# Sparse attention and a soft mixture of experts on one core: engine programs in a block, or in the main body

## The chip, the core and the metric

The kernel runs on one core of a Trainium2 chip. The core has five engines with an instruction stream each: PE (matrix products; its weight loads are shown as PEld), DVE (vector), ACT (activation functions), POOL and SP. They run on their own and meet through semaphores only. Transfers between the chip's memory and the core's are issued by SP, ACT and POOL and carried out by 16 DMA engines. The metric is the device time of one execution in microseconds (us).

## The reference

```python
# q, k, v: [8, 8, 576, 64]
scores = scale * np.matmul(q, k.transpose(0, 1, 3, 2))
mask_plain = (rel >= 0) & (rel < window)                  # window = 32
mask_dil = (rel >= 0) & (rel < window * dilation) & (rel % dilation == 0)   # dilation = 4
scores = np.where(masks, scores, -1e9)      # first 4 heads plain, last 4 dilated
attn = softmax(scores);  attn_out = np.matmul(attn, v)
x = attn_out.transpose(0, 2, 1, 3).reshape(4608, 512)
logits = x @ phi                            # 32 slots: 8 experts of 4
d = softmax over the 4608 tokens;  slot_input = d.T @ x
for e in range(8):
    slot_out[e] = np.maximum(slot_input[e] @ w1[e], 0.0) @ w2[e]
c = softmax over the 32 slots;     return c @ slot_out      # [4608, 512] f32
```

## The kernel before

The attention is done in eight units (two batches of one kind of head each). For each unit POOL issues the loads of q, k and v into one of three staging buffers (`stg`), PE transposes them and ACT copies the result to `TT`; PE forms the scores, ACT their exponentials, DVE the masks; PE multiplies by the values, DVE divides, PE transposes again and forms the logits. The experts' weights, 32 MB in f32, are fetched through POOL's queue all along, into buffers as they come free (`WD`, `stg`, `TT`), and cast to bf16 on the way. At the end the two products of each expert run on PE, the outputs are formed in `WD` and `stg` by ACT (L1062) and DVE (L1061), and they are stored by SP, a few by ACT (L1056).

The whole program is recorded first. A call of `op` adds a step with its engine, what it reads and writes, a cost and a key; `P.schedule` gives each engine an order from these; `P.emit` then writes the instructions, one engine after the other. Nothing of this order depends on where `emit` writes them.

`emit` (L276) takes `eng_of`, which gives for each engine something that is called with a function and runs it with that engine (used as a decorator). Inside, every step's waits are written ahead of it and its semaphore is raised behind it (`c_pe`, `c_act` and so on; each transfer has its own).

Before, `eng_of` holds the decorators of a `Block` (L1167). A block gives every engine a stretch of program of its own: in the listing of the built program each engine has one `UnconditionalBranch` from the main body into its stretch (L314) and one at its end to the block's end (L1177). SP has two stretches, the second for the waits on the stores, with a branch between them (L1172). At the block's end stands a barrier of all five engines: PE, ACT, DVE and SP each drain and add one to a gathering semaphore; POOL drains, waits until it holds four, and adds four to a releasing semaphore, which each of the others waits for and counts down. All instructions of this barrier are shown under L1177. A barrier of the same form, with L1192 as its line, stands at the head of the program, before the block, and is written by the language, not by the kernel.

`s_out` (L416) lists the semaphores of the 18 stores. The last thing that SP does ahead of the closing barrier is to wait for each of them (L1174 and L1175). Other engines don't wait for the stores; they meet SP in the closing barrier.

The lines that matter below: L462, L516 and L532 (the first loads and ACT's first instruction), L495 (weight loads by POOL), L1056 (stores), L1175 (waits for the stores), L1177 (branches to the end and closing barrier), L1192 (opening barrier).

Of the kernel before, what the change touches and what calls it, by code (L numbers as in the profile page):

```python
# [327 lines left out]
def bass_dilated_sliding_attn__then__soft_moe_slots_kernel(  # L328
# [10 lines left out]
    A = es.enter_context  # L339
    P = Prog()  # L340
# [75 lines left out]
    s_out = []  # L416
# [575 lines left out]
    COLS, d_ = [], 0  # L992
# [156 lines left out]
    def filler(n):  # L1149
        t = tile(psum, 1)  # L1150

        def pe(te):
            for _ in range(n):
# [11 lines left out]

    P.schedule(filler, FILL)

    blk = A(nc.Block())
    P.emit(nc, {"pe": blk.tensor, "act": blk.scalar, "dve": blk.vector,
                "pool": blk.gpsimd, "sp": blk.sync})  # L1170

    @blk.sync  # L1172
    def _(sp):
        for d_ in s_out:  # L1174
            sp.wait_ge(d_.sem, d_.val)  # L1175

    es.close()  # L1177
    return nc
# [28 lines left out]
```

## Time and profile before

| | us |
|---|---|
| median of 3 runs (lowest, highest) | 176.54 (176.09, 176.54) |
| the profiled execution, its own time | 176.33 |
| its span, first to last instruction | 174.6 |
| busy: PE, DVE, ACT, POOL | 129.6, 110.4, 96.2, 65.3 |

The span runs from the first instruction of the kernel's program to the end of its last; the time of an execution also holds what lies around it, here 1.7 us. In the profile's 40 slices (4.4 us each) a digit is the busy share in tenths. A row of the chain of waits gives start, length and what the time went to; a row of waits gives the time waited in all, how often, and the longest. An engine's name with a q is its sequencer: waits, branches, drains and the issuing of transfers, which don't count as busy. The trace also holds the single instructions with their starts in nanoseconds, and the semaphore events with theirs, including those of the program that the launch puts around the kernel's own.

### The profile page before, as it was taken

To read this page: it belongs to the slowest core of one execution; us is meant where nothing else is said; L and a number is where in the kernel's file an instruction comes from. 1 tells how busy PE (TensorE), PEld (TensorE's weight loads), DVE (VectorE), ACT (ScalarE), POOL (GpSimd) and SP (SyncE) were. 2 spreads that over 40 slices of the span, in tenths; PEclk is the share of its full clock that TensorE was granted. 3 is DMA by queue.
4 is the path that set the end of the run, shared out by engine and by line. 5 is a ranking of instruction groups with operands and counts; after the bars stand their busy time and mean duration, and the time that the engine had idled before them with its cause. 6 is when DMAs were issued, how large, how long until landed. Compare 5 with 4: busy or idle time off the path is not lost.

```text
span 174.6 us, 5117 instructions
## 1 busy us (share of the span) xinstructions
PE 129.6 (74%) x2234; PEld 99.3 (57%) x2235; DVE 110.4 (63%) x259; ACT 96.2 (55%) x147; POOL 65.3 (37%) x111
## 2 busy tenths in 40 slices
PE   0057778989898999997989899978599856589000
PEld 0056668968686977885977797765454413333000
DVE  6620199299869899969789979996401102499200
ACT  2324743797978769797768696763101101589300
POOL 7980668404964033952020769498000000000000
PEclk9999996999999999999999999999957999999855
DMA  5999998999999999999999999999999999999997
GB/s 178 252 213 213 220 232 187 222 209 214 229 222 199 219 209 216 237 203 206 221 207 218 212 216 216 216 220 214 212 207 208 206 196 197 290 347 404 452 420 300
DMA packets 12693, 41.28 MB, mean 236 GB/s; under 512 B 2208, under 2 KB 8864, under 8 KB 9120
## 3 DMA queue, kind: packets, MB, share of 16 engines
q0 software_dynamic: 8128, 30.41, 86.6%
q1 hardware_dynamic: 2912, 8.98, 13.3%
q10 hardware_dynamic: 1632, 1.57, 2.7%
q8 instruction: 17, 0.28, 0.6%
q14 instruction: 4, 0.03, 0.0%
HBM read 61.93 MB, written 9.44 MB: 409 GB/s over the span
## 4 chain that ended last, share of the span: by engine, by line
PE 34%; DMA 23%; ACT 13%; DVE 13%; POOL 5%; issue 3%; ACTq 1%; POOLq 0%
DMA TT<-in_moe_w_dram 17%; PE ps L636 8%; PE ps L642 7%; DMA stg<-in_v_dram 6%; ACT PT L695 5%; DVE XB L753 4%; PE ps L713 4%; ACT WD L1062 4%; PE ps L742 4%; PE ps L688 4%; DVE PT L703 4%; PE ps L797 3%; PE ps L770 3%; ACT TT L670 3%; POOL TT L495 2%
## 5 line engine op out<-in xcount | busy, mean ns | idle before, releaser
L695 ACT ACTIVATE PT<-ps 128x768 bf16<-128x768 f32 x48 | 36.9, 819 | 11.5 <-PE ps L688 11.2
L670 ACT ACTIVATE TT<-ps 128x864 f32<-128x864 f32 x32 | 27.9, 901 | 17.6 <-PE ps L642 9.0
L753 DVE TENSOR_TENSOR XB<-ps,RV 96x768 bf16<-96x768 f32 x32 | 30.1, 944 | 0.4
L642 PE MATMUL ps<-ident,stg 96*128 96x96 bf16 x288 | 16.9, 225 | 12.7 <-DMA stg<-in_v_dram 12.0
L718 DVE COPY VN<-ps 128x768 bf16<-128x768 bf16 x32 | 17.1, 543 | 9.8 <-PE ps L713 9.5
L642 PEld LDWEIGHTS ps<-ident,stg 96*128 96x128 bf16 x288 | 15.4, 109 | 13.5 <-DMA stg<-in_v_dram 12.2
L742 PE MATMUL ps<-VN,PT 128*128 128x65 bf16 x384 | 17.3, 195 | 2.8 <-DVE XB L753 1.7
L688 PE MATMUL ps<-TT 64*128 64x96 bf16 x384 | 16.5, 213 | 3.2 <-ACT PT L695 1.2
L1062 ACT ACTIVATE WD<-ps,rtok 128x256 f32<-128x256 f32 (+1 forms) x22 | 10.5, 554 | 13.9 <-PE ps L1079 12.6
L713 PE MATMUL ps<-ident,TT 128*128 128x128 bf16 x192 | 17.1, 228 | 1.0 <-issue 0.3
L609 POOL COPY stg<-stg 96x576 f32<-96x576 f32 x24 | 16.8, 702 | 1.5
L742 PEld LDWEIGHTS ps<-VN,PT 128*128 128x128 bf16 x384 | 14.5, 99 | 4.2 <-DVE XB L753 1.9
L688 PEld LDWEIGHTS ps<-TT 64*128 64x128 bf16 x384 | 10.3, 98 | 8.7 <-ACT PT L695 2.3
L703 DVE TENSOR_TENSOR PT<-PT,mask_d 128x768 bf16<-128x768 bf16 x24 | 14.0, 616 | 0.0
L770 PE MATMUL ps<-ident,XB 96*128 96x96 bf16 x192 | 12.2, 211 | 2.2 <-DVE XB L753 1.5
L713 PEld LDWEIGHTS ps<-ident,TT 128*128 128x128 bf16 x192 | 11.8, 102 | 3.3 <-issue 1.1
L703 DVE TENSOR_TENSOR PT<-PT,mask_p 128x768 bf16<-128x768 bf16 x24 | 12.6, 544 | 0.2
L448 POOL DMA_DIRECT2D stg<-in_q_dram x8 | 4.1, 525 | 21.7 <-PE ps L642 21.7
L770 PEld LDWEIGHTS ps<-ident,XB 96*128 96x128 bf16 x192 | 9.5, 101 | 4.2 <-DVE XB L753 2.8
L636 PE MATMUL ps<-ident,stg 96*128 96x96 bf16 x216 | 11.2, 212 | 0.0
L783 ACT ACTIVATE XT<-ps 128x576 bf16<-128x576 bf16 x16 | 10.0, 651 | 1.6 <-PE ps L770 1.4
L636 PEld LDWEIGHTS ps<-ident,stg 96*128 96x128 bf16 x216 | 10.5, 102 | 0.4
(99 smaller groups left out, 204.0 us busy)
## 6 DMA issues: line engine op xcount, KB each, us to landing
WD<-in_moe_w_dram POOLq DMA_DIRECT2D x6, 1024.0 KB, 25.9
stg<-in_moe_w_dram POOLq DMA_DIRECT2D x5, 1024.0 KB, 31.6
stg<-in_q_dram POOLq DMA_DIRECT2D x10, 288.0 KB, 17.7
stg<-in_k_dram POOLq DMA_DIRECT2D x10, 288.0 KB, 19.4
stg<-in_v_dram POOLq DMA_DIRECT2D x10, 288.0 KB, 21.6
out_dram<-WD SPq DMA_DIRECT2D x2, 1024.0 KB, 5.3
out_dram<-WD SPq DMA_DIRECT2D x1, 2048.0 KB, 8.5
out_dram<-stg SPq DMA_DIRECT2D x1, 2048.0 KB, 11.1
```

Of the source, the lines that this page charges most:

```text
L636: i_ = t.transpose(bankb2(pt, a)[:, 96 * kk:96 * kk + 96], il_ap(u, j, a)[:, 128 * kk:128 * kk + 128], ident[0:96, 0:96])
L642: i_ = t.transpose(bankb2(pt, a)[:, 96 * kk:96 * kk + 96], two[:, c, :], ident[0:96, 0:96])
L670: return ac.activation(d, sv, ACTF.Copy)
L688: i_ = t.matmul(pair(sc)[:, hx, QB * x:QB * x + QB], win(u, 1, h01, blk_, bpar)[64 * hx:64 * hx + 64], win(u, 0, h01, blk_, bpar)[64 * hx: ...
L695: op("act", lambda ac: ac.activation(sbt(pt)[:, 0:768].rearrange("p (x n) -> p x n", x=2), pair(sc)[:, :, 0:384], ACTF.Exp, scale=SCALE), ...
L703: return dv.tensor_tensor(p_, p_, m.unsqueeze(1).to_broadcast([128, 2, 384]), AluOp.mult)
L713: i_ = t.transpose(bankb(pv)[:, 128 * m:128 * m + 128], win(u, 2, h01, m, bpar), ident[:, :])
L718: op("dve", lambda dv: dv.tensor_copy(sbt(vn)[:, :, :, 0:64], bankb(pv)[:, 0:768].rearrange("p (m x d) -> p m x d", m=6, x=2)), r=[pv], w= ...
L742: i_ = t.matmul(pair(po)[:, bk, 65 * po_:65 * po_ + 65], sbt(pts[i])[:, o_:o_ + 128], sbt(vn)[:, m, half, 0:65], start=True, stop=True)
L753: op("dve", lambda dv: dv.tensor_tensor(sbt(xb)[:].rearrange("p m (x h d) -> p h x m d", x=2, h=2)[:, h01], pv()[:, :, :, 0:64], sbt(rv)[: ...
L770: i_ = t.transpose(bankb(px)[:, QB * m:QB * m + QB], sbt(xb)[:, m, 128 * x:128 * x + 128], ident[0:QB, 0:QB])
L1062: return en.activation(d_, s_, ACTF.Copy, scale=k_)
```

## The change

The block is gone. `eng_of` now holds, for each engine, a function that calls what `emit` hands it with `nc.tensor`, `nc.scalar` and so on, so that the instructions are written into the main body, right behind the opening barrier. The waits for the stores are written to SP there, after everything else.

```diff
-    blk = A(nc.Block())
-    P.emit(nc, {"pe": blk.tensor, "act": blk.scalar, "dve": blk.vector,
-                "pool": blk.gpsimd, "sp": blk.sync})
-
-    @blk.sync
-    def _(sp):
-        for d_ in s_out:
-            sp.wait_ge(d_.sem, d_.val)
+    def body(eng):
+        return lambda f: f(eng)
+
+    P.emit(nc, {"pe": body(nc.tensor), "act": body(nc.scalar), "dve": body(nc.vector),
+                "pool": body(nc.gpsimd), "sp": body(nc.sync)})
+    for d_ in s_out:
+        nc.sync.wait_ge(d_.sem, d_.val)
```

In the listing of the built program this takes away the branches (L314, L1172, L1177) and the closing barrier: a drain and a semaphore wait on each of PE, ACT, DVE and SP, a drain and two semaphore instructions on POOL. The order of all other instructions on each engine is the same, and so are their waits, but for the pairing of SP's waits for the stores: one instruction can carry two waits, and the 18 are packed on nine instructions and the branch before, on nine instructions after. The opening barrier stays.

## The prediction

> **What bounds the kernel now.** I read the page first, for the span and for what is busy in each stretch; then the chain that ended last, towards its end; then who waited on SP's queue; then the line of the closing barrier by itself; last the single records at both edges of the span, because a change that touches only the edges is priced there. The page:
>
> ```profile
> span 174.6 us, 5117 instructions
> ...
> PE   0057778989898999997989899978599856589000
> ...
> POOL 7980668404964033952020769498000000000000
> ...
> DMA  5999998999999999999999999999999999999997
> ```
>
> The DMA row is at 9 from the second slice to the last but one: the transfers bound the kernel, with PE, DVE and ACT working behind them. POOL's row is empty from the 29th slice on (122 us), PE's in the last three. So at the end there is nothing but stores. The chain's late pieces say the same:
>
> ```profile
> 118.58 2.24 POOL TT L495 x3
> 120.82 30.43 DMA TT<-in_moe_w_dram
> ...
> 161.83 0.58 ACTq L1177
> 162.41 0.58 ACT stg L1062
> ```
>
> The last weights land at 151.2, the last eviction ends at 163.0, and the chain has no computing piece after it. What fills the remaining 11.6 us of the span is in SP's waits and the store's own row:
>
> ```profile
> out_dram<-stg SPq DMA_DIRECT2D x1, 2048.0 KB, 11.1
> ```
>
> ```profile
> SPq L1175 <- DMA out_dram<-WD: 5.5, 2, 4.8
> SPq L1175 <- DMA out_dram<-stg: 4.8, 1, 4.8
> ...
> SPq L1177 <- PEq L1177: 0.2, 1, 0.2
> ```
>
> SP issued the last store at 163.01 and 11.1 us later it landed; SP (L1175) waited for it. The last row is the closing barrier (L1177, the line of the block's end). That line by itself, times in ns:
>
> ```profile
> L1177 POOLq EVENT_SEMAPHORE  x2: 17/17/17, 174.4 to 174.5; - x2
> L1177 POOLq DRAIN  x1: 37206/37206/37206, 117.0 to 117.0; - x1
> L1177 PEldq DRAIN  x1: 707/707/707, 160.7 to 160.7; - x1
> L1177 ACTq DRAIN  x1: 1592/1592/1592, 161.4 to 161.4; - x1
> L1177 DVEq DRAIN  x1: 1276/1276/1276, 161.4 to 161.4; - x1
> L1177 SPq COMPARE_BRANCH  x1: 33/33/33, 174.2 to 174.2; - x1
> L1177 SPq DRAIN  x1: 7/7/7, 174.4 to 174.4; - x1
> L1177 SPq EVENT_SEMAPHORE  x1: 17/17/17, 174.5 to 174.5; - x1
> ```
>
> Four engines reach the end at 117 to 161 us and sit in the barrier; only SP comes late. The single records give the order to the nanosecond: SP's wait for the last store passes at 174.138, its branch is at 174.203, its drain at 174.363, POOL collects at 174.396 and releases at 174.479, SP passes at 174.521, PE's release (0.051 long) ends the span at 174.583.
>
> The trace also keeps semaphore events beyond the span. In the profiled run of 176.33 us they are: nine steps of a second barrier, of the launch program around the kernel (its own semaphore), at 174.822, 174.857, 175.072, 175.116, 175.139, 175.237, 175.275, 175.311 and 175.357; then some 250 semaphores set back in five groups until 175.923; then nine more steps, 176.177 to 176.535. The group that starts first (175.264) follows the fifth step, so the fifth engine turns the pass round. I read the order as PE, ACT, POOL, DVE, SP and back: the group set back last and slowest is PE's (PE's release record is 0.051 against 0.017 for ACT, POOL and SP), and SP, whose records are among the shortest, is fifth. That reading is inferred from these times, not labelled in the trace.
>
> **The change part by part.** *Branches into the block, one for each engine:* 0. The trace has no record on L314 and one branch in all, SP's at the end. From the opening barrier's release to the first instruction SP takes 0.083 us (0.733 to 0.816) and ACT 0.076; two of SP's plain waits at the end are 0.059 to 0.065 apart, so at most 0.02 is there to save. POOL takes 0.686 (0.692 to 1.378), but its next loads also follow at 0.638 and 0.507: descriptor work. Bounds: 0 to 0.6 if all of POOL's gap but an SP-like step were the branch; I take 0, nearest to SP's row.
>
> [...]
>
> *Instruction order:* none moves. PE, ACT, DVE and POOL keep every instruction and wait; on SP the eighteen waits for stores ride on nine wait instructions and the branch before, on nine wait instructions after, and the last store's wait stays in the last of these. No DMA is moved past another in any queue. DMA-bound time up to 174.138: unchanged.
>
> *Four early drains* (0.7, 1.6, 1.3 and 37.2 us): 0, hidden behind SP's wait for the stores. The last of them ends at 163.02 (161.427 + 1.592), 11.1 us before 174.138; with that cover gone ACT's 1.6 us would count.
>
> *Closing barrier on SP:* branch, drain, collect, release: from 174.138 to 174.521 = **0.38 us**, all on the path, since nothing but SP's last wait is behind it. With PE's longer release the span itself loses 174.583 − 174.166 (SP's last wait with its 0.028) = 0.42.
>
> *The barrier behind the span:* before, all five engines come to it together, so its forward pass is paid after 174.58: SP's step is at 175.139, 0.618 after SP left the kernel at 174.521. After the change PE, ACT, DVE and POOL have been at it since 163 or earlier; the forward pass up to SP is done and only SP's own way to its step is left. That way is hidden in before (SP's step follows DVE's by 0.023, so SP may have been ready long before). Bounds: 0 to 0.60. Nearest rows: PE, first in the pass and waiting for nobody, needs 0.24 from its release (174.583 to 174.822); ACT at most 0.32 (174.542 to 174.857). I take PE's 0.24, hence 0.60 − 0.24 = **0.36 us** saved, between 0 and 0.60. The way back, the setting back and the last barrier all follow SP's step and only shift.
>
> [...]
>
> **Sum:** 0.38 + 0.36 = 0.74 us off 176.33: **175.59** for a run like the profiled one. The runs shown have the median 176.54, 0.21 above it, which would give 175.80; I forecast **175.7**, between the two (0.4% below).
>
> **Rivals.**
> *Only the closing barrier goes* (176.33 − 0.38 = 175.95, or 176.16 from the median): SP's own way to the second barrier is as long as the 0.60 that it had. For it: POOL's step came 0.215 after ACT's, so some engine does have some 0.5 us of its own there. Against: POOL is the odd one, and PE's row has 0.24. That gain is 0.2%.
>
> *The start gains as well* (0.686 − 0.166, DVE's way into its first instruction, = 0.5 us more, 175.2): POOL's 0.686 is partly the branch, and the first load starts the whole stream earlier. Against: SP's 0.083.
>
> *Slower: POOL walks on too early.* Before, POOL's drain holds it from 116.95 to 154.16 while its software queue still brings the last weights. Without it POOL enters the launch program's end steps at 121.6, in the middle of the 30.43 us for TT on the chain. Whatever makes its step late by 0.2 us there would run beside POOL's descriptors. If that slows the 33 us of loads from 118 to 151 by more than 0.74 / 33 = 2.2%, it decides; at 4% the time is 176.33 + 1.32 − 0.74 = 176.9. For it: POOL's drain is the only thing that kept it still. Against: POOL's descriptors are issued by 121.64, and a program that must not end early would itself drain first.
>
> *The pages shift.* PE's idle steps that wait for nothing (82.67, 108.62) sit at one place in every 256 instructions of its compiled stream, a fetch of 16 KB each. Should the block's markers be instructions, PE loses one ahead of the body and each such stop moves by one instruction of about 0.02 us: 17 pages, ±0.3 us. Against: five markers on SP and two on ACT cost the same 0.08 us. I give it no chance of its own; it widens the range.
>
> **How the numbers follow.** Forecast 0.68; closing barrier alone 0.20; start as well 0.06; slower 0.06. From no change this kernel's measurement can tell about 0.3%, 0.53 us (its three runs differ by 0.45). The forecast lies 0.2 beyond that, so a part of it, 0.06, falls within 0.3%, as do nearly all of the closing barrier's cases: same 0.68 × 0.09 + 0.18 = 0.24. Faster: 0.62 + 0.06 + 0.02 = 0.70. Slower: 0.06. The range: from 176.33 − 0.98 = 175.35, less 0.2 for a part of the start, 175.15, up to 176.54 − 0.37 = 176.17 with 0.1 for the spread of runs, 176.3. It leaves out the slower case and the full gain at the start.
>
> **What would show it.** The span near 174.17, ending with SP's wait for the last store and no L1177 record; the store still landing 11.1 us after an issue near 163.0; SP's step of the second barrier 0.2 to 0.3 after its last wait, the four others' steps long before; first load still at 1.38. Wrong: SP's step 0.6 after its last wait (only the closing barrier), or the last TT load landing later than 151.2 and POOL's steps at 121 (slower), or PE's first matmul earlier than 10.9 (the start).

## The result, and the profile after

| | before | changed |
|---|---|---|
| median (lowest, highest), 4 runs each | 176.54 (176.09, 176.89) us | 174.95 (174.81, 175.33) us |
| ratio, 95% interval | | 0.9915 [0.9887, 0.9942] |
| profiled execution, its span | 176.33, 174.6 us | 174.98, 173.7 us |

The changed kernel is faster by 0.85%, about twice the forecast, and below its range. The page of the changed kernel, the rows that were shown of before:

```profile
span 173.7 us, 5106 instructions
...
PE   0057788999898799999998899987869895889000
...
POOL 6980668120995004980202674949400000000000
...
DMA  5999999999999999999999999999999999999998
```

DMA is as full as it was, and PE and POOL still have nothing to do at the end. The trace holds 11 records fewer. The closing barrier had 12 (SP's branch, five drains, the releases of SP, ACT, DVE and PE, two semaphore instructions on POOL), and one product that the trace of before lacked is there. Who waited on SP's queue in the changed kernel, and the line of its waits for the stores (ns):

```profile
SPq L1174 <- DMA out_dram<-WD: 5.5, 2, 4.9
SPq L1174 <- DMA out_dram<-stg: 4.8, 1, 4.8
```

```profile
L1174 SPq EVENT_SEMAPHORE  x9: 28/28/28, 163.0 to 173.7; - x9
```

The two waits for transfers are as long as before; the row that waited for PE in the closing barrier is gone, and the ninth wait, at 173.7, is the last record of the span. The store's row reads 11.1 us to landing, unchanged.

The start, in order of time (start, length, what, and in brackets the idle time before it), first of before and then of the changed kernel:

```profile
0.82 0.37 SPq L516 DMA_DIRECT2D WD<-in_moe_w_dram  x1
...
1.38 0.65 POOL L462 DMA_DIRECT2D stg<-in_q_dram  x1 [0.86 <-POOLq L1192]
```

```profile
0.82 0.37 SPq L516 DMA_DIRECT2D WD<-in_moe_w_dram  x1
...
1.38 0.64 POOL L462 DMA_DIRECT2D stg<-in_q_dram  x1 [0.86 <-POOLq L1191]
```

Both first loads stand where they stood: the branches into the block cost nothing.

The single records and semaphore events behind SP's wait for the last store tell where most of the time went. A step is one raise of the launch program's semaphore; each engine makes one on the way forward, in a fixed order with SP last, and the other four make one each on the way back. In the changed kernel SP's wait passes at 173.718. By then the barrier has its steps at 161.153 (PE), 162.699 (ACT), 162.738 (POOL) and 162.782 (DVE) behind it; SP's is at 173.860, and the way back ends at 174.023. (The trace doesn't label the steps with engines; the names are borne out by main_pe_wait, main_pool_wait and two more traces below.) The semaphores are set back until 174.588, and the last barrier ends at 175.169. From SP's last wait:

| us from SP's wait for the last store | before | changed | less |
|---|---|---|---|
| to SP's branch and on to its drain (0.065 + 0.160), less a wait's own 0.065 | 0.160 | 0 | 0.160 |
| rest of the closing barrier, to SP's release | 0.223 | 0 | 0.223 |
| to SP's step of the launch program's barrier | 0.618 | 0.142 | 0.476 |
| from there to the last step of its last barrier | 1.396 | 1.309 | 0.087 |
| sum | 2.397 | 1.451 | 0.946 |

(The first row's 0.065 is kept in the second: 0.065 + 0.158 from SP's drain to its release.) The profiled runs differ by 176.33 − 174.98 = 1.35. The time from SP's wait for the last store to the last step of the last barrier is called the edge from here on: 2.397 before, 1.451 in the changed kernel. Of the 1.35, 0.95 is the edge; 0.42 is the last store, for which SP's wait passed at 173.718 instead of 174.138; and 0.02 goes off again, since, counted from the start of the span, the recorded times end 0.205 and 0.189 ahead of the last step. Whether these 0.42 belong to the change is what the experiments had to tell.

### The profile page after: what moved, and what is told of

Read it like the earlier page. It is cut to its first block, busy times and chain, and to the rows that moved or that the text cites. A ratio compares the mean times of both kernels' runs of the same rounds, so it can differ in the third digit from the quotient of the medians.

```text
span 173.7 us, 5106 instructions
## 1 busy us (share of the span) xinstructions
PE 133.1 (77%) x2235; PEld 103.0 (59%) x2235; DVE 109.6 (63%) x259; ACT 96.6 (56%) x147; POOL 65.7 (38%) x111
## 4 chain that ended last, share of the span: by engine, by line
PE 31%; DMA 22%; DVE 18%; ACT 14%; POOL 5%; issue 2%; ACTq 0%; POOLq 0%
DMA TT<-in_moe_w_dram 16%; PE ps L636 8%; PE ps L642 8%; DVE XB L753 6%; DMA stg<-in_v_dram 6%; ACT PT L695 5%; DVE PT L703 4%; ACT WD L1062 4%; PE ps L713 4%; PE ps L688 3%; PE ps L797 3%; DVE VN L718 3%; POOL TT L495 3%; PE ps L742 3%; ACT TT L670 3%
## 5 line engine op out<-in xcount | busy, mean ns | idle before, releaser
L642 PE MATMUL ps<-ident,stg 96*128 96x96 bf16 x288 | 18.7, 239 | 12.1 <-DMA stg<-in_v_dram 11.8
L642 PEld LDWEIGHTS ps<-ident,stg 96*128 96x128 bf16 x288 | 17.4, 118 | 12.7 <-DMA stg<-in_v_dram 12.0
L742 PEld LDWEIGHTS ps<-VN,PT 128*128 128x128 bf16 x384 | 15.0, 101 | 2.6 <-DVE XB L753 1.5
L636 PE MATMUL ps<-ident,stg 96*128 96x96 bf16 x216 | 12.5, 225 | 0.2 <-DVE XB L753 0.2
L636 PEld LDWEIGHTS ps<-ident,stg 96*128 96x128 bf16 x216 | 11.7, 109 | 0.8 <-DVE XB L753 0.4
L751 DVE RECIPROCAL RV<-ps 96x12 f32<-96x12 f32 x32 | 6.8, 217 | 7.3 <-PE ps L742 7.3
## 6 DMA issues: line engine op xcount, KB each, us to landing
out_dram<-stg SPq DMA_DIRECT2D x1, 2048.0 KB, 11.1
```

The lines of the kernel that those rows point to most:

```text
L636: i_ = t.transpose(bankb2(pt, a)[:, 96 * kk:96 * kk + 96], il_ap(u, j, a)[:, 128 * kk:128 * kk + 128], ident[0:96, 0:96])
L642: i_ = t.transpose(bankb2(pt, a)[:, 96 * kk:96 * kk + 96], two[:, c, :], ident[0:96, 0:96])
L742: i_ = t.matmul(pair(po)[:, bk, 65 * po_:65 * po_ + 65], sbt(pts[i])[:, o_:o_ + 128], sbt(vn)[:, m, half, 0:65], start=True, stop=True)
```

## The experiments

The theory: everything that the change saves lies behind SP's wait for the last store (0.95 us less edge), and the time ahead of it varies from run to run. The rivals: POOL's drain, waiting beside the last weights, slowed them; or the missing branches and markers make the body faster.

**The barrier put back without the block** (main_barrier).

```diff
         nc.sync.wait_ge(d_.sem, d_.val)
+    nc.all_engine_barrier()
```

> The changed kernel with the all-engine barrier put back at its end, without the block: no branches, no markers. Edge theory (all of the gain lies behind SP's wait for the last store: the closing barrier and the forward pass of the launch program's barrier; the 0.4 us by which the last store landed earlier in the changed kernel is run to run): the time from that wait to the last step of the launch program's barriers goes back from 1.45 to 2.40 us, the median to that of before within 0.3%, 176.0 to 176.6. Rival (the body is faster without branches and markers, through another place of the instruction pages): the edge comes back but the last store keeps landing near 173.7, so 175.9.

176.08 us, ratio to before 0.9997 [0.9961, 1.0033]. The barrier's line in its trace (ns):

```profile
L1175 POOLq EVENT_SEMAPHORE  x2: 17/17/17, 173.8 to 173.8; - x2
L1175 POOLq DRAIN  x1: 36057/36057/36057, 117.4 to 117.4; - x1
...
L1175 SPq DRAIN  x1: 7/7/7, 173.7 to 173.7; - x1
L1175 SPq EVENT_SEMAPHORE  x1: 17/17/17, 173.9 to 173.9; - x1
```

All that was in before is there again but the branch: SP's drain follows its last wait by 0.065, where it was 0.225. The edge is 2.205 us; the 0.16 of SP's branch is most of what it lacks of 2.397. The last store's wait passed at 173.665 in the profiled run, earlier than in the changed kernel. That is where the rival had it, but this run was the fastest of ten (175.68, the median is 176.08), so the sign decides nothing. The ratio does: with the barrier alone the gain is gone, within the interval. A body faster by the 0.64 us that the measured gain (1.59 between the medians) has beyond the edge would have given a ratio near 0.995, outside the interval.

**POOL's drain alone** (main_pool_drain).

```diff
         nc.sync.wait_ge(d_.sem, d_.val)
+    nc.gpsimd.drain()
```

> The changed kernel with a drain on POOL alone at the end of its program. Edge theory: POOL's drain ends near 154, 20 us before SP, so nothing: 174.95, edge 1.45 us. Rival (POOL's drain, waiting from 117 to 154 while its queue brings the last weights, slows these): the last weights land 0.4 to 0.6 us later, 175.4 to 175.6, and the last store's wait passes near 174.1.

174.94 us, ratio 0.9927 [0.9889, 0.9964]. The drain is as long as before:

```profile
L1175 POOLq DRAIN  x1: 35139/35139/35139, 118.2 to 118.2; - x1
```

It held POOL until 153.4, the last weights landed at 150.17 (150.39 in the changed kernel), and the edge is 1.451 us. So POOL's drain costs nothing here: it is over 20 us before SP's last wait passes.

**The block without POOL's drain** (block_no_pool_drain).

```diff
-    blk = A(nc.Block())
+    blk = A(nc.Block(no_gpsimd_drain=True))
```

> The kernel before, with its block, branches and closing barrier, but without POOL's drain in it (the barrier is of semaphores only). Edge theory: the closing barrier and the forward pass stay behind SP's wait, so 176.2 to 176.6, and from that wait to the last step 2.2 to 2.4 us. Rival (POOL's drain slows the last weights): 0.4 to 0.6 less, 175.9 to 176.1, with the last store's wait near 173.7.

175.94 us against 176.13, ratio 0.9969 [0.9935, 1.0004]: by its time inconclusive. 175.94 lies in the range that was given to the rival, but both ranges were drawn from the slower runs of before known then; against the 176.13 of before here, the interval holds both no change and the rival's 0.4 us less. In the trace POOL's drain is gone, while PE, ACT, DVE and SP still drain, each now ahead of its semaphore instruction. SP's wait passed at 173.985, not near 173.7, and the last weights landed at 150.73, later than in main_pool_drain, where POOL drains; the edge is 2.425 us. A single trace can't settle 0.4 us, since the last store's wait varies by more than that among the traces below. Against the rival stands main_pool_drain, which is as fast as the changed kernel.

**All five engines come late, without a closing barrier** (main_all_wait).

```diff
         nc.sync.wait_ge(d_.sem, d_.val)
+    for eng in (nc.tensor, nc.scalar, nc.vector, nc.gpsimd):
+        eng.wait_ge(s_out[-1].sem, s_out[-1].val)
```

> The changed kernel, with PE, ACT, DVE and POOL also waiting for the last store at the end of their programs: no closing barrier, but all five come to the launch program's barrier together. Edge theory: SP's step of that barrier comes some 0.6 us after its last wait instead of 0.14, so 0.45 to 0.5 us more than the changed kernel, 175.4. If the gain were the closing barrier alone, 174.95.

175.54 us, ratio 0.9954 [0.9925, 0.9984]. SP's step comes 0.639 after its wait, the edge is 2.024. That lies between the kernel before and the changed one: the forward pass of the launch program's barrier is a part of the gain, beside the closing barrier.

**Which engine makes that pass long** (main_pe_wait, main_pool_wait: the same line for PE or for POOL alone).

```diff
         nc.sync.wait_ge(d_.sem, d_.val)
+    nc.tensor.wait_ge(s_out[-1].sem, s_out[-1].val)
```

> The changed kernel with PE alone also waiting for the last store. If PE is first in the launch program's barrier and the others follow in a row: PE's step 0.24 after the last store's wait, ACT, POOL, DVE and SP behind it by some 0.035 each, SP's step at 0.38 to 0.42 (0.14 without the wait, 0.64 with all four waits). If the order were another and SP not behind PE: 0.14.

The wait passed at 174.214; the steps followed at 174.463, 174.497, 174.535, 174.579 and 174.602: PE's own comes 0.249 after SP's wait, then the other four in a row, SP's at 0.388.

> The changed kernel with POOL alone also waiting for the last store. If POOL's own way to its step is what is long (0.215 and 0.287 behind ACT's where all came together): POOL's step some 0.56 after the last store's wait, DVE's and SP's right behind, SP's at 0.63, nearly all that the waits of all four cost (0.64). If the pass is paid by hops alike, 0.25 to 0.3.

Two steps, 161.435 and 162.986, came early; the third followed the wait (174.069) by 0.567, the next two by 0.043 and 0.024 more, SP at 0.634. So PE stands first and POOL third, and with POOL alone held back SP's step is as late as with all four (0.634 and 0.639): POOL's own way, 0.57 us, is what makes the pass long. ACT and DVE follow from two traces in which DVE's last eviction ended after ACT's. In main_third they end at 162.754 and 162.400, and the fourth step is at 162.904, the second at 162.519; in main_pool_drain they end at 162.965 and 162.621, with the fourth step at 163.115 and the second at 162.741. So ACT is second, DVE fourth, and SP last. The times, 175.77 and 175.90, are single runs and carry nothing; the edges, 1.750 and 2.030, do.

**A barrier without drains** (main_sem_barrier).

```diff
         nc.sync.wait_ge(d_.sem, d_.val)
+    nc.all_engine_barrier(sem_only=True)
```

> The changed kernel with an all-engine barrier of semaphores alone at its end, no drain on any engine. Edge theory: the same as with the drains in the barrier, since these are covered: edge 2.2 us, 0.9 times of before to 1.0, median 175.9 to 176.1, ratio 0.998 to 1.000. Rival (drains cost 0.3 us ahead of the last store): edge 2.2 us but the last store's wait at 173.7, 175.7, ratio 0.997.

176.28 us against 176.29, ratio 0.9999 [0.997, 1.0029], edge 2.244, against 2.205 with the drains (main_barrier). The drains are covered; what costs is that the five meet. The 0.3 us that the drains were suspected to cost ahead of the edge did not show: the ratio is 0.9999, and the rival's 0.997 is the last value of the interval.

**The changed kernel again, and before against itself** (main_again, main_third, block_copy; no edit).

> The changed kernel once more, for the part ahead of the edge: with the edges of the traces so far (2.19 us from SP's last wait to the end of the counted time before, 1.26 after) the medians so far put the last store's wait at 173.94 in before (31 runs), 174.07 with the barrier put back, and at 173.68 to 173.72 in the four kernels without it. Edge theory: those 0.3 us are spread of runs, so changed and before differ by 0.93 us, ratio 0.9947. Rival (the barrier with its drains, POOL's among them, also costs 0.3 us ahead of the last store): 1.2 us, ratio 0.993.

> The changed kernel a third time, beside an unchanged copy of the kernel before. Edge theory: the edge measured in the traces is 2.40 us before and 1.45 changed, the time ahead of it is the same in both, so 0.95 us less, ratio 0.9946, whatever the chip; the 1.6 us of the first measurement (4 runs of each) and the 1.2 us of the kernel with POOL's drain were 0.95 and the spread of the medians. Rival (something ahead of the last store also gets faster by 0.2 to 0.6 us): ratio 0.991 to 0.9935.

> The kernel before, unchanged, against itself: what a difference of nothing looks like here. Both theories: 1.000; how far its median lies from that of the other runs of before is the spread that a comparison of this size has, 0.1 to 0.4 us.

main_again 175.56 against 176.29, ratio 0.9949 [0.9923, 0.9975]. main_third 175.09 against 176.06, ratio 0.9946 [0.9932, 0.9959]. block_copy 176.08, ratio 1.0000 [0.998, 1.0021]. The narrowest of the three measurements of the change, main_third, puts it at 0.54%, 0.95 us with an interval from 0.72 to 1.20. The difference of the edges, 0.946, lies in its middle; that they agree to the hundredth is luck, since the edge of before itself was 2.397 in one trace and 2.364 in the other. Of the rival's 0.991 to 0.9935 the interval leaves only the end next to the theory. In block_copy the closing barrier is there as ever:

```profile
SPq L1175 <- DMA out_dram<-stg: 4.8, 1, 4.8
...
SPq L1177 <- PEq L1177: 0.2, 1, 0.2
```

and yet its last store's wait passed at 173.379, the earliest of all. The runs together:

| kernel | last store's wait | SP's step after it | edge | ratio [95%] |
|---|---|---|---|---|
| before | 174.138 | 1.001 | 2.397 | |
| block_copy | 173.379 | 0.998 | 2.364 | 1.0000 [0.998, 1.0021] |
| block_no_pool_drain | 173.985 | 1.067 | 2.425 | 0.9969 [0.9935, 1.0004] |
| main_sem_barrier | 173.886 | 0.854 | 2.244 | 0.9999 [0.997, 1.0029] |
| main_barrier | 173.665 | 0.841 | 2.205 | 0.9997 [0.9961, 1.0033] |
| main_all_wait | 173.684 | 0.639 | 2.024 | 0.9954 [0.9925, 0.9984] |
| main_pool_wait | 174.069 | 0.634 | 2.030 | |
| main_pe_wait | 174.214 | 0.388 | 1.750 | |
| main_pool_drain | 173.748 | 0.142 | 1.451 | 0.9927 [0.9889, 0.9964] |
| changed | 173.718 | 0.142 | 1.451 | 0.9915 [0.9887, 0.9942] |
| main_again | 173.879 | 0.137 | 1.445 | 0.9949 [0.9923, 0.9975] |
| main_third | 173.689 | 0.142 | 1.452 | 0.9946 [0.9932, 0.9959] |

Each row is one trace, and the ratio is of all its runs. The second column spreads over 0.84 us without following the ending; the fourth follows it. No ending that was tried has a shorter edge than that of the changed kernel: SP's step is 0.14 after its wait for the last store, and what comes after that is not the kernel's.

## Why the prediction was wrong

*What bounds the kernel, and where the change acts*: right: the last store's wait follows no ending within its spread, and the gain that repeats is as large as what the edge lost. (The prediction's 151.2 for the last weights is where the chain lets PE go on; the last packet landed at 150.90.)

*Branches into the block, 0*: right; the first loads are at 0.82 and 1.38 in both traces. POOL's 0.686 from its release to its first load is 0.687 without the branch (0.693 to 1.380); that descriptor work fills it was the author's estimate; no run shows what it consists of. The 0.1 kept for the start, and its rival, fall. The prediction's sign for it, a first product earlier than 10.9, does appear (10.74), but it tells nothing: over the twelve traces the first product starts between 10.39 and 11.69, and in block_copy, which has the branches, at 10.86.

*Drains, 0*: right; POOL's alone costs nothing (main_pool_drain), and a barrier without any is no faster than before (main_sem_barrier).

*Closing barrier on SP, 0.38*: right, 0.383. That 0.16 of it is the branch at SP's end was in the records and not singled out; main_barrier, which has the barrier without the branch, shows it.

*The barrier behind the span, 0.36 between 0 and 0.60*: the first step that failed, a term that was mis-sized. Its mechanism is right (main_all_wait, main_pool_wait, main_pe_wait), but SP's own way is 0.142, not PE's 0.24, so 0.476 is saved. Taking the nearest row's engine for SP was the fault: PE's semaphore record in the barrier is three times as long as SP's (0.051 against 0.017 us, L1177), as the prediction itself used to tell them apart. What SP waited for in before was POOL, whose step (175.072) came 0.576 after the end of its release (174.496), the same 0.57 that main_pool_wait shows.

*"The way back, the setting back and the last barrier … only shift"*: nearly; they were 0.087 shorter (1.396 to 1.309). 0.055 of that is the way from SP's step to PE's last, 0.218 before and 0.163 in the changed kernel, and nearly all of it is the first hop behind SP: 0.098 before, 0.044 in the changed kernel. In the table's traces that hop is 0.097 or 0.098 wherever DVE's step came just ahead of SP's, and 0.043 or 0.044 in the four where SP alone came late. Why is open. The other 0.032 lies behind the way back and follows no ending: from its last step to the end it takes 1.140 to 1.178 in the first eight traces and 1.146 or 1.147 in those four.

*Sum, 0.74*: 0.946 in the traces, so the two terms were 0.2 short. That alone would not have left the range: taken off 176.33 it gives 175.38. The recorded median of 174.95 is 0.43 below that. The repeats give 0.73 and 0.97 between the medians (175.56 against 176.29, 175.09 against 176.06), and main_pool_drain, with the same ending, 1.19 (174.94 against 176.13), not 1.59; the intervals of main_again and main_third end at 1.36 and 1.20. The first four runs of before have the highest median of its four samples (176.54; the others 176.06 to 176.29), those of the changed kernel the lowest of its three (174.95, 175.09, 175.56). So I put the excess of the first four runs, 0.64 us, down to spread. It was not traced further, and the first interval, which ends at 0.9942, just leaves out the edge's 0.9946: its cause stays open.

*The range*: the second step that failed. It had 0.1 for the spread of runs on its upper side and nothing on its lower one, though the three runs shown of before already differed by 0.45. Against other runs of before the changed kernel's 175.09 lies below 175.15 as well, since before itself was at 176.06 there.

*Rivals*: the closing barrier alone was 0.56 short (0.383 of 0.946), and main_all_wait, which takes away only that barrier, shortens the edge by 0.373. Slower by POOL walking on early fell as to its effect: the last weights landed at 150.39 (150.90 before). Whether POOL's end steps ran beside its last loads cannot be told, since its step waits for ACT's (162.7). The shift of PE's pages (17 fetches of 16 KB in both traces, q8 of the page) left no mark larger than the spread of the last store's wait, 0.84 us; no run shifted it by itself.

## What to carry to other kernels

In this kernel one engine alone is late at the end. A meeting of all five behind it cost 0.38 us by itself and 0.48 more, because it held the other four back from the launch program; when they go ahead, the late one has only its own way to make, 0.142 us for SP. Look for the same in a kernel whose last act is one engine's wait. Price the end by the events behind the span, not by the span alone: the barrier's part of the span was 0.42 us (174.583 − 174.166), and the edge lost 0.95. And compare medians over enough runs: four of each gave 0.85% with an interval that ended at 0.58%, seventeen and five gave 0.54%.

## What the runs showed of the hardware

- The way from the end of the kernel to an engine's step in the launch program's barrier: SP 0.14 us (the changed kernel), PE 0.25 (main_pe_wait), POOL 0.57 (main_pool_wait), each counted from SP's wait for the last store. Where the engines are ready, a hop of the pass forward takes 0.023 to 0.044 (main_pe_wait).
- SP's branch with a wait on it (COMPARE_BRANCH in the trace) took 0.160 us from its start to the next instruction (0.156 in block_copy); from SP's last plain wait to the instruction behind it, it is 0.065 (before, main_barrier).
- POOL's drain waited 37.2 us in before, 36.1 in main_barrier and 35.1 in main_pool_drain while its queue brought the last weights, and no delay of these shows: they landed at 150.12 to 150.90 in the four traces with it and at 150.34 to 150.99 in the eight without.
